# Linear attention with a routed expert layer: turns 4 to 19 of the attention in another order, their output rows turned in two halves

## The chip, the cores and the metric

The kernel runs on one core of a Trainium2 chip. Its engines are TensorE (PE, whose weight loads are listed as PEld), VectorE (DVE), ScalarE (ACT), GpSimd (POOL) and SyncE (SP), which issues most of the transfers. The metric is the device time of one execution in microseconds (us), less is better.

## The reference

A linear attention with a forget gate per channel (4 batches, 8 heads, 768 steps, 48 channels a head) makes one row of 384 numbers for each of 3072 tokens. An expert layer follows: each token goes to the one of 8 experts with the largest gate logit.

```
f = 1 / (1 + exp(-f_logit))
for t in range(S):
    state = f[:, :, t, :, None] * state + einsum('bhd,bhe->bhde', k[:, :, t], v[:, :, t])
    y[:, :, t] = einsum('bhd,bhde->bhe', q[:, :, t], state)
x = y as rows of tokens (3072 x 384)
logits = x @ w_gate; e_idx = argmax(logits)
for each expert e, on its tokens:
    out = gate_w * sigmoid(x @ w_output_gate)[e] * (relu(x @ w1[e]) @ w2[e])
```

## The kernel before

**Attention.** The steps are cut into chunks of 128 tokens: 4 batches of 6 chunks are 24 chunks in a row, and the loop `for t in range(last + 1)` makes one *turn* for each. Heads stand in pairs on the partitions (NP = 4 pairs of 64 rows). A turn holds work on several chunks, since each chunk goes through a pipeline:

- `pre(t + 2, ...)`, `pre(t + 3, "s")`: gates and their running products two or three chunks ahead. `s` and `f` are sigmoids on ACT from the loaded `f_t` (f into the single PSUM buffer `f_ps`), `scan_p` and `scan_i` are scans on DVE over `f_ps`, `mul_q` and `mul_k` multiply q and k by them on POOL, `ends` is a small copy on ACT.
- `qk(t)`: scores of the chunk on PE into two `a_ps` tiles. `mask` copies them to `at`: one half by ACT and then POOL (affine_select), the other by DVE.
- `kn_tr(t)`, `evac_kn(t)`: k with tokens on partitions, turned on PE and copied by ACT. The last chunk of a batch (t = 5, 11, 17, 23) has neither, nor a state product.
- `out_y(t - 1)` = `out_state` (q with the carried state) and `out_at` (scores with v) on PE. Their sums stand in half a PSUM bank each: `y_ps[0]` in the bank `two`, `y_ps[1]` in the bank `one`.
- `state(t - 1)`: product of k and v on PE into `s_ps`, the other half of the bank `one`. `state_upd` on DVE adds it to the carried state.
- `evac_y`: two copies on ACT of the outputs into `xt`. `x_tr(t - 2)` turns them into rows of tokens on PE (the right operand `turn` also yields the gate logits, 112 columns in all), and `evac_x` copies these on ACT.
- `route`, `slots` (every second or fourth turn): which expert each token goes to, on DVE, with a few small products on PE into the other half of the bank `two` (the rank products). `scatter`: POOL writes the rows of 128 tokens into the list of their experts in `xs_dram`, one scatter a turn from turn 7 on, more from turn 20 (`T_END`) on. With the first 16 tiles counted (`T_TOP`), a vote on DVE names the largest expert, whose w1 is then loaded.

The order in which the program is written is the order on each engine: `chain` ties every instruction of PE, DVE, ACT and POOL to the one before it on its engine. The transfers of SP run through one queue, in which the next one is issued when the eighth before it has landed. `clear` writes empty rows into the lists ahead of the scatters; only tiles that are known to stand elsewhere are declared apart from them, and the scatter of tile 3 waits for the second set of four writes. The tile framework lets an instruction wait for readers and writers of the same PSUM bank on other engines: `state_upd` waits for the copy of `one`, the rank products wait for that of `two`.

**Hand-over and experts.** In the last turn the reload of the first 256 tokens of the largest expert (`first_x`) waits for the first 16 scatters. `x_early_turn` and `x_early` turn and split them (DVE, ACT), and `mm1_early` is the first expert product (tile `h_ps`). From there on PE multiplies for the experts, one after another.

Of the kernel before, what the change touches and what calls it, by code (L numbers as in the profile page):

```python
# [21 lines left out]
C = 128  # L22
NCH = S // C
NP = H // 2
# [6 lines left out]
EARLY = 256  # L31
T_TOP = 16
T_END = 20
AHEAD = 8
KC = DM // 128
KF = F // 128
# [96 lines left out]
def attention(ctx, tc, nc, k, kpool, rt, q01, k01, f01, q23, k23, f23, v, wg, xs_dram, r, ex):  # L133
# [104 lines left out]
    def hot(t):  # L238
        return 0 <= t < len(order)
# [37 lines left out]
    def state(t):  # L277
        b, c = order[t]
        if c == NCH - 1:
            return  # L280
        for h in range(H):
            g, r0 = h // 2, 64 * (h % 2)
            nc.tensor.matmul(s_ps[r0:r0 + 64, g, 0:D], kn[t][:, 64 * h:64 * h + 64],  # L283
                             v_t[b][:, c, 64 * h:64 * h + D],
                             start=(h < 2), stop=(h >= 6), skip_group_check=True)

    def state_upd(t):
        b, c = order[t]
        if c == NCH - 1:
            return  # L290
        end = r.pend[:, t * NP:t * NP + NP].unsqueeze(2).broadcast_to([128, NP, D])
        scomp[t] = states[t % 2]
        new, kv = scomp[t][:, :, 0:D], s_ps[:, :, 0:D]
        if c == 0:
            nc.vector.tensor_tensor(out=new, in0=kv, in1=end, op=ALU.mult)
        else:
            nc.vector.tensor_tensor(out=stmp, in0=kv, in1=scomp[t - 1][:, :, 0:D], op=ALU.add)
            nc.vector.tensor_tensor(out=new, in0=stmp, in1=end, op=ALU.mult)
# [29 lines left out]
    def evac_y(t, halves=(1, 0)):  # L328
        if t not in xt:
            xt[t] = wk.tile([128, NP, C], F32, name="xt")  # L330
        for i in halves:
            nc.scalar.copy(out=xt[t][:, i::2, :], in_=yps[t][i])

    def x_tr(t):

        xps[t] = psB.tile([128, 512], F32, name="x_ps")[:, 0:NP * XW].rearrange("p (g e) -> p g e", e=XW)
        for g in range(NP):
            nc.tensor.matmul(xps[t][:, g, :], xt[t][:, g, :], turn[:, g, :], start=(g == 0), stop=(g == NP - 1))  # L338

    def evac_x(t):  # L340
        if t % 4 == 0:
# [22 lines left out]
    dq, pq = [], []  # L364
# [110 lines left out]
    def pre(t, *names):  # L475
        if hot(t):
            for nm in names:
                if nm not in done[t]:
                    done[t].add(nm)
                    pre_of[t][nm]()  # L480
# [26 lines left out]
    for gi, n in enumerate(RG):  # L507
        ends[t0 + n - 1] = (gi, t0, n)
        t0 += n
    for t in range(last + 1):  # L510
        ready = len(pq)
        more = 1 if t < T_END else 0

        fill(more)
        if hot(t - 2):
            evac_y(t - 2, (1,))
        if t not in (0, 2):
            pre(t + 2, "f")
        if hot(t - 2):
            evac_y(t - 2, (0,))  # L520
            state_upd(t - 2)
        if t == 2:
            pre(4, "f")
            pre(3, "ends")
        pre(t + 1, "mul_k")
        if t + 1 == last:
            done_sb.close()
            ex.open_early()
        fill(more)
        if t > 1:  # L530
            pre(t + 2, "scan_p")
        qk(t)
        mask(t, 1)
        mask(t, 0)
        pre(t + 2, "scan_p", "scan_i")
        fill(more)
        kn_tr(t)
        if t == 0:
            warm_up(nc, k, one, 6)
        if t == last:  # L540
            run_pq(ready)
        if hot(t - 2):
            x_tr(t - 2)
        evac_kn(t)
        pre(t + 2, "mul_q", *(("ends",) if t != 1 else ()))
        if hot(t - 2):
            evac_x(t - 2)
        if t == last:
            route(*ends[t - 2])
            drain()  # L550
        fill(more)
        if T_END <= t < last:
            fill(8)
        pre(t + 3, "s")
        if t == last:
            done_ps.close()
            ex.open_early_psum()
        if hot(t - 1):
            out_y(t - 1)
        if hot(t - 1):  # L560
            state(t - 1)
        if t == last:
            hand_over()
            break
        run_pq(ready)
        if t >= T_END:
            pre(t + 2, "mul_k")
        if t >= T_SCAT:
            scatter(1 if t < T_END else 2)

        b, c = divmod(t - 3, NCH)
        if t >= 3 and b + 2 < B and c in (0, 2, 4):
            if c == 4:
                load(b + 2, [("v", 0, 2)])
            load(b + 2, [("kq" if t == 3 else "fkq", c, c + 2)])
            if t == 3:
                ex.clear(3)
            if c == 4:
                load(b + 2, [("v", i, i + 2) for i in range(2, NCH, 2)])
        fill(2 if more else 10)  # L580
        fill(2 * more)
        if t - 2 in ends:
            route(*ends[t - 2])
        if t >= T_END:
            scatter(2)
            if len(ex.apart) == T_TOP:
                ex.tokens_in(0, 0, EARLY // TS)
                ex.load_rest(0)
        if t + 1 == last:
            drain()  # L590
            assert ex.xq
            ex.split(1, 0, 0)
# [600 lines left out]
```

## Time and profile before

| what | value |
|---|---|
| median of 3 runs | 352.92 us (352.49 to 352.97) |
| the profiled execution | 353.29 us, span from first to last instruction 351.6 us |
| PE busy | 339.4 us, 97% of the span |
| DVE, ACT, POOL busy | 250.0, 202.0, 209.8 us (71%, 57%, 60%) |
| turns of the attention | the first product of turn 0 at 9.2 us, of turn 4 at 25.75 us, of turn 20 at 97.16 us |

The shares are means over stages with different limits. The change touches the stretch from 25.75 to 97.16 us, which is why the rows below are cut by turn. Times in them count from the first instruction.

### The profile page before, as it was taken

What the parts mean: (1) busy time and instruction counts of PE and PEld (TensorE: products, weight loads), DVE (VectorE), ACT (ScalarE), POOL (GpSimd) and SP (SyncE); (2) the same over time, 40 slices, a digit from 0 to 9 for tenths busy, and PEclk for the clock granted to TensorE, in tenths of its full rate; (3) what the DMA queues carried; (4) which work ended last, traced back from release to release, by engine and by line L of the source; (5) the groups of instructions that cost most, each with busy time, mean ns of one, the idle gap of its engine ahead of it and who ended that gap; (6) DMA issues with size and microseconds to landing.
All of it is one profiled execution on the core that took longest, in us unless ns stands there. A gap on an engine that the chain in (4) does not pass through costs nothing.

```text
span 351.6 us, 8639 instructions
## 1 busy us (share of the span) xinstructions
PE 339.4 (97%) x3039; PEld 317.5 (90%) x3039; DVE 250.0 (71%) x495; ACT 202.0 (57%) x507; POOL 209.8 (60%) x250
## 2 busy tenths in 40 slices
PE   7899999999999899999999999999999999999991
PEld 2698988898988799999989999999999999999991
DVE  6998989898998676668766675766667666655600
ACT  3576866776766561455754752672673672775410
POOL 8786698999988461000674475276276276278521
PEclk9999999999999999999999999999999999999997
DMA  8999999999928927997683393495484484420101
GB/s 254 350 359 357 296 301 261 261 279 261 276 71 278 297 85 129 282 234 183 185 243 86 110 284 84 139 245 132 139 223 138 140 217 143 140 76 28 60 31 38
DMA packets 75204, 67.63 MB, mean 192 GB/s; under 512 B 30813, under 2 KB 69481, under 8 KB 75152
## 3 DMA queue, kind: packets, MB, share of 16 engines
q1 hardware_dynamic: 70576, 57.34, 60.4%
q0 software_dynamic: 4576, 9.66, 8.1%
q8 instruction: 26, 0.43, 0.5%
q14 instruction: 26, 0.21, 0.2%
HBM read 54.04 MB, written 13.46 MB: 192 GB/s over the span
## 4 chain that ended last, share of the span: by engine, by line
PE 84%; DMA 4%; DVE 3%; issue 3%; POOL 2%; ACT 1%; SPq 0%; POOLq 0%; DVEq 0%; ACTq 0%
PE h_ps L810 32%; PE y_ps L830 25%; PE x_ps L338 5%; PE a_ps L250 5%; PE y_ps L844 5%; PE two_ps L318 3%; PE kn_ps L267 3%; PE one_ps L318 2%; PE two_ps L310 2%; PE one_ps L283 2%; DMA xs_dram<-xn,slot 2%; DMA f_t<-in_f 1%; DVE p L214 1%; DMA first_x<-xs_dram 1%; POOL out L874 1%
## 5 line engine op out<-in xcount | busy, mean ns | idle before, releaser
L863 POOL DMA_INDIRECT out<-yr,dst x83 | 90.3, 1088 | 70.8 <-ACT yr L862 44.9
L810 PE MATMUL h_ps<-xh,w1h 128*128 128x400 f32 (+6 forms) x192 | 65.4, 341 | 0.0
L810 PE MATMUL h_ps<-xh,w1l 128*128 128x400 f32 (+6 forms) x192 | 65.4, 340 | 0.0
L810 PE MATMUL h_ps<-xl,w1h 128*128 128x400 f32 (+6 forms) x192 | 65.3, 340 | 0.0
L815 DVE SCALAR_TENSOR_TENSOR hl<-h_ps,hh 128x256 fp32r<-128x256 f32 (+6 forms) x72 | 39.0, 544 | 32.8 <-ACT hh L814 32.6
L814 ACT ACTIVATE hh<-h_ps 128x256 fp32r<-128x256 f32 (+6 forms) x72 | 34.5, 482 | 42.6 <-PE h_ps L810 41.4
L830 PE MATMUL y_ps<-hh,w2h 128*128 128x256 f32 (+4 forms) x168 | 56.1, 334 | 0.0
L830 PE MATMUL y_ps<-hl,w2h 128*128 128x256 f32 (+4 forms) x168 | 56.0, 334 | 0.0
L830 PE MATMUL y_ps<-hh,w2l 128*128 128x256 f32 (+4 forms) x168 | 56.0, 334 | 0.0
L673 DVE TENSOR_TENSOR w1l<-w1r,w1h 128x768 fp32r<-128x768 f32 x31 | 29.7, 959 | 16.7 <-ACT w1h L672 16.5
L810 PEld LDWEIGHTS h_ps<-xh,w1h 128*128 128x128 f32 x192 | 36.1, 188 | 0.8
L810 PEld LDWEIGHTS h_ps<-xl,w1h 128*128 128x128 f32 x192 | 36.1, 188 | 0.7
L810 PEld LDWEIGHTS h_ps<-xh,w1l 128*128 128x128 f32 x192 | 36.1, 188 | 0.7
L228 POOL TENSOR_TENSOR q_t<-q_t,p 128x512 f32<-128x512 f32 x24 | 30.5, 1272 | 3.5 <-DVE p L214 2.3
L830 PEld LDWEIGHTS y_ps<-hh,w2h 128*128 128x128 f32 x168 | 31.7, 189 | 0.7
L830 PEld LDWEIGHTS y_ps<-hh,w2l 128*128 128x128 f32 x168 | 31.7, 189 | 0.7
L830 PEld LDWEIGHTS y_ps<-hl,w2h 128*128 128x128 f32 x168 | 31.7, 189 | 0.7
L355 POOL DMA_INDIRECT xs_dram<-xn,slot x24 | 24.5, 1022 | 10.8 <-issue 5.9
L673 DVE TENSOR_TENSOR w2l<-w2r,w2h 128x768 fp32r<-128x768 f32 x31 | 29.6, 954 | 1.4 <-ACT w2h L672 0.6
L777 ACT CAST xh<-xr 128x400 fp32r<-128x400 f32 (+6 forms) x24 | 12.2, 517 | 31.2 <-DVE xr L771 30.1
L250 PE MATMUL a_ps<-q_t,k_t 64*128 64x128 f32 x384 | 27.9, 285 | 2.1 <-DVE k_t L225 1.1
L225 POOL TENSOR_TENSOR k_t<-k_t,i 128x512 f32<-128x512 f32 x22 | 28.2, 1280 | 2.6 <-DVE i L221 1.4
(168 smaller groups left out, 738.5 us busy)
## 6 DMA issues: line engine op xcount, KB each, us to landing
w1r<-in_w SPq DMA_DIRECT2D x32, 384.0 KB, 4.0
w2r<-in_w SPq DMA_DIRECT2D x32, 384.0 KB, 3.5
v_t<-in_v SPq DMA_DIRECT2D x12, 512.0 KB
xs_dram<-empty SPq DMA_DIRECT2D x8, 401.0 KB, 10.5
f_t<-in_f SPq DMA_DIRECT2D x6, 512.0 KB, 4.0
q_t<-in_q SPq DMA_DIRECT2D x6, 512.0 KB
k_t<-in_k SPq DMA_DIRECT2D x6, 512.0 KB, 10.2
f_t<-in_f SPq DMA_DIRECT2D x12, 192.0 KB, 9.3
```

The lines of the kernel that those rows point to most:

```text
L225: eng.tensor_tensor(out=k_t[i][:, :, sl], in0=k_t[i][:, :, sl], in1=d["i"], op=ALU.mult)
L228: nc.gpsimd.tensor_tensor(out=q_t[i][:, :, sl], in0=q_t[i][:, :, sl], in1=d["p"], op=ALU.mult)
L250: nc.tensor.matmul(aps[t][par][:, g, :], k_t[b % 2][r, g, sl], q_t[b % 2][r, g, sl], start=(g == 0), stop=(g == NP - 1))
L318: nc.tensor.matmul(yps[t][g % 2][r0:r0 + 64, g // 2, :], v_t[b][:, c, 64 * h:64 * h + 64], at[t][:, h % 2, g, :], start=((first or c == 0) ...
L338: nc.tensor.matmul(xps[t][:, g, :], xt[t][:, g, :], turn[:, g, :], start=(g == 0), stop=(g == NP - 1))
L355: i = nc.gpsimd.indirect_dma_start(out=xs_dram, out_offset=bass.IndirectOffsetOnAxis(ap=r.slot[:, t:t + 1], axis=0), in_=xn[t // 4][:, t % ...
L673: (eng or self.nc.vector).tensor_tensor(out=to(lo), in0=of(t), in1=to(hi.bitcast(F32)), op=ALU.subtract)
L810: nc.tensor.matmul(ps[:, 0:n], a[:, c, cs], b, start=(i == 0), stop=(i == 3 * KC - 1))
L814: nc.scalar.activation(out=hi, in_=ps[:, 0:n], func=AF.Relu)
L815: nc.vector.scalar_tensor_tensor(out=lo, in0=ps[:, 0:n], scalar=0.0, in1=hi.bitcast(F32), op0=ALU.max, op1=ALU.subtract)
L830: self.nc.tensor.matmul(self.ys[d][:, c0:c0 + n], a, b, start=(f == 0 and i == 0 and part == 0), stop=(f == KF - 1 and i == 2), skip_group ...
L863: self.other_rows(self.nc.gpsimd.indirect_dma_start(out=self.out.rearrange("n (q w) -> (n q) w", q=NQ), out_offset=bass.IndirectOffsetOnAx ...
```

## The change

Turns 4 to 19 (the fifth to the twentieth) run `next_turn` in place of the old body, which becomes `old_turn` and serves turns 0 to 3 and 20 to 23. In `next_turn` the outputs of the chunk before stand right behind `qk`, then the state's product, and the rows and k are turned last. The copies of outputs and the state's update stand in the same turn as their products, the copy of the bank `one`, which the state's product shares, second. `f` is computed a turn earlier. `closed` keeps the old body from doing an update a second time. `x_tr(t, 2)` makes each product in two halves of 64 tokens, 64 weight columns each, into the partitions 0 to 63 and 64 to 127.

```diff
+T_NEXT = 4
...
-    def x_tr(t):
+    def x_tr(t, parts=1):
...
+        n = C // parts
         for g in range(NP):
-            nc.tensor.matmul(xps[t][:, g, :], xt[t][:, g, :], turn[:, g, :], start=(g == 0), stop=(g == NP - 1))
+            for a in range(0, C, n):
+                nc.tensor.matmul(xps[t][a:a + n, g, :], xt[t][:, g, a:a + n], turn[:, g, :], start=(g == 0),
+                                 stop=(g == NP - 1), skip_group_check=True)
...
-    for t in range(last + 1):
-        ready = len(pq)
-        more = 1 if t < T_END else 0
-
+    def old_turn(t, ready, more):
         fill(more)
-        if hot(t - 2):
+        if hot(t - 2) and t - 2 not in closed:
             evac_y(t - 2, (1,))
...
-        if hot(t - 2):
+        if hot(t - 2) and t - 2 not in closed:
             evac_y(t - 2, (0,))
             state_upd(t - 2)
...
+    def next_turn(t, ready):
+
+        if t - 2 not in closed:
+            evac_y(t - 2)
+            state_upd(t - 2)
+        pre(t + 1, "mul_k")
+        pre(t + 2, "f", "scan_p")
+        qk(t)
+        mask(t, 1)
+        mask(t, 0)
+        pre(t + 2, "mul_q", "ends")
+        pre(t + 3, "s")
+        fill(1)
+        out_y(t - 1)
+        state(t - 1)
+        pre(t + 2, "scan_i")
+        fill(2)
+        evac_y(t - 1, (0, 1))
+        state_upd(t - 1)
+        closed.add(t - 1)
+        pre(t + 3, "f")
+        x_tr(t - 2, 2)
+        kn_tr(t)
+        evac_x(t - 2)
+        evac_kn(t)
...
+        if T_NEXT <= t < T_END:
+            next_turn(t, ready)
+        else:
+            old_turn(t, ready, more)
```

Below, rows of the built programs in their order on an engine; line numbers after the change are 1, 4 or more higher.

PE in turn 9, before (from `qk` to `state`; a_ps are the scores, kn_ps the turned k, x_ps the turned outputs, one_ps and two_ps the banks):

```order
L250 MATMUL a_ps<-q_t_99,k_t_101 128x128 x8
L267 MATMUL kn_ps<-ident,k_t_101 128x128 x4
L338 MATMUL x_ps<-turn,xt 128x112 x4
L310 MATMUL two_ps<-q_t_99,state_107 64x128 x2
...
L318 MATMUL two_ps<-at,v_t 64x128 x2
...
L283 MATMUL one_ps<-v_t,kn 64x48 x8
```

PE in turn 9 after the change:

```order
L251 MATMUL a_ps<-q_t_99,k_t_101 128x128 x8
L311 MATMUL two_ps<-q_t_99,state_107 64x128 x2
...
L319 MATMUL two_ps<-at,v_t 64x128 x2
...
L284 MATMUL one_ps<-v_t,kn 64x48 x8
L341 MATMUL x_ps<-turn,xt 64x112 x8
L268 MATMUL kn_ps<-ident,k_t_101 128x128 x4
```

The turning of rows and of k moved from behind the scores to the end of the turn, and the rows' four products became eight of 64 partitions.

ACT over one turn, before (from the copy of masked scores of turn 9 on; start_p is `s`, f_ps is `f`):

```order
L255 ACTIVATE at<-a_ps 128x512
L275 COPY kn<-kn_ps 128x512
L231 COPY pend<-p 128x4
L345 COPY lgp<-x_ps 128x64
L346 COPY xn<-x_ps 128x384
L202 ACTIVATE start_p_176<-f_t_102 128x4
L204 COPY p<-start_p_176 128x1
L332 COPY xt<-one_ps 128x2x128
L209 ACTIVATE f_ps<-f_t_102 128x4x127
L332 COPY xt<-two_ps 128x2x128
```

ACT over the same turn after the change:

```order
L256 ACTIVATE at<-a_ps 128x512
L232 COPY pend<-p 128x4
L203 ACTIVATE start_p_176<-f_t_102 128x4
L205 COPY p<-start_p_176 128x1
L333 COPY xt<-two_ps 128x2x128
L333 COPY xt<-one_ps 128x2x128
L210 ACTIVATE f_ps<-f_t_102 128x4x127
L349 COPY lgp<-x_ps 128x64
L350 COPY xn<-x_ps 128x384
L276 COPY kn<-kn_ps 128x512
```

`s` moved ahead of both copies of the outputs, `f` behind them, and the copies of the rows and of k to the end, in the order of PE.

## Rows read from the trace of the kernel before

**Rows 1.** Windows from turn to turn: length, busy (instructions), clock, DMA share, GB/s.

```profile
47.93:52.56 4.63, 4.63 (x80) 4.18 (x76) 4.04 (x7) 3.31 (x10) 4.42 (x5) 1.00 1.08 326
...
61.90:66.07 4.17, 4.17 (x64) 3.60 (x60) 3.89 (x8) 3.23 (x10) 3.92 (x5) 1.00 1.11 275
...
74.74:79.58 4.84, 4.84 (x85) 4.36 (x81) 3.81 (x7) 3.50 (x11) 4.66 (x6) 1.00 1.08 274
...
84.21:88.71 4.50, 4.32 (x77) 3.79 (x73) 3.91 (x7) 2.76 (x9) 4.30 (x5) 1.00 1.09 276
...
92.89:97.16 4.27, 4.27 (x69) 3.97 (x67) 3.81 (x7) 3.45 (x11) 4.08 (x6) 1.00 0.91 282
97.16:101.79 4.63, 4.63 (x80) 4.17 (x77) 4.01 (x13) 3.19 (x10) 3.72 (x5) 1.00 0.20 74
```

**Rows 2.** Timeline of PE in turn 9: start, length, engine, line, work.

```profile
49.02 0.66 PE L267 MATMUL kn_ps<-ident,k_t 128*128 128x128 f32 x4
49.52 1.04 PE L338 MATMUL x_ps<-turn,xt 128*128 128x112 f32 x8
50.49 0.33 PE L310 MATMUL two_ps<-q_t,state 64*64 64x128 f32 x2
...
51.09 0.44 PE L318 MATMUL two_ps<-at,v_t 128*64 128x128 f32 x4
...
51.58 0.39 PE L318 MATMUL two_ps<-at,v_t 128*64 128x128 f32 x4
...
52.01 0.62 PE L283 MATMUL one_ps<-v_t,kn 128*64 128x48 f32 x16
```

**Rows 3.** Line of the state's product: ns of one, shortest, median, longest.

```profile
L283 PE MATMUL one_ps<-v_t,kn x320: 206/222/222, 15.8 to 115.4; 128*64 128x48 f32 x160
```

**Rows 4.** Timeline of PE in turn 17; in brackets idle time and releaser.

```profile
85.56 1.15 PE L338 MATMUL x_ps<-turn,xt 128*128 128x112 f32 x8 [0.18 <-ACT xt L332]
```

**Rows 5.** Timeline of POOL: scatters, mul_k (L225), mul_q (L228).

```profile
58.41 1.01 POOL L355 DMA_INDIRECT xs_dram<-xn,slot  x1 [1.13 <-DMA q_t<-in_q]
59.45 1.29 POOL L225 TENSOR_TENSOR k_t<-k_t,i 128x512 f32<-128x512 f32 x1
...
65.63 1.27 POOL L228 TENSOR_TENSOR q_t<-q_t,p 128x512 f32<-128x512 f32 x1
...
69.94 1.27 POOL L228 TENSOR_TENSOR q_t<-q_t,p 128x512 f32<-128x512 f32 x1
...
80.45 1.01 POOL L355 DMA_INDIRECT xs_dram<-xn,slot  x1 [0.56 <-DVE misc L297]
...
94.50 1.28 POOL L225 TENSOR_TENSOR k_t<-k_t,i 128x512 f32<-128x512 f32 x1
```

**Rows 6.** Timeline of ACT around s(18) (L202) in turn 15.

```profile
77.51 0.49 ACT L346 COPY xn<-x_ps 128x384 f32<-128x384 f32 x1
78.15 0.21 ACT L202 ACTIVATE start_p<-f_t 128x4 f32<-128x4 f32 x1
...
79.49 0.37 ACT L332 COPY xt<-one_ps 128x256 f32<-128x256 f32 x1 [0.85 <-PE one_ps L283]
```

**Rows 7.** Timeline of SP: issue of the loads of f for turns 18, 19.

```profile
66.91 1.21 SPq L190 DMA_DIRECT2D f_t<-in_f  x2
```

**Rows 8.** Chain that ended last, at the hand-over: start, length, what.

```profile
106.60 6.56 DMA xs_dram<-xn,slot
...
114.78 3.59 DMA first_x<-xs_dram
```

**Rows 9.** Timeline at the hand-over: SP's issue of w1, PE's last and first products.

```profile
103.32 2.86 SPq L647 DMA_DIRECT2D w1r<-in_w  x4
...
118.58 0.28 PE L310 MATMUL f_ps<-q_t,state 64*64 64x128 f32 x2
...
119.43 0.38 PE L810 MATMUL h_ps<-xah,w1h 128*128 128x256 f32 x1 [0.55 <-ACT xah L777]
```

More of the change, by code (lines that the diff above doesn't have):

```diff
@@ L561, in attention @@
             state(t - 1)
+    def next_turn(t, ready):
[22 more added lines that the diff above has]
+        evac_kn(t)
+    closed = set()
+    for t in range(last + 1):
+        ready = len(pq)
+        more = 1 if t < T_END else 0
+        if T_NEXT <= t < T_END:
+            next_turn(t, ready)
+        else:
+            old_turn(t, ready, more)
         if t == last:
```

## The prediction

> **What bounds the kernel now.** I read the sums by turn first: one window from the first product of a turn to that of the next. In a full turn TensorE (PE) is busy for the whole window, 4.63 of 4.63 us, at a granted clock of 1.00, while VectorE (DVE), ScalarE (ACT) and GpSimd (POOL) are busy for 4.04, 3.31 and 4.42 us [rows 1]. So the order of work on PE sets the pace of turns 4 to 19, and the reader should look for three things: what a turn costs PE, where PE waits, and what else would stop it if it were quicker.
>
> The timeline of PE in turn 9 gives the cost by block, from start to start: qk 1.09, kn_tr 0.50, x_tr 0.97, out_state 0.60, out_at 0.92, state 0.55, together 4.63 us (the turn's ends are those of its window) [rows 1, 2]. Nothing waits in it. PE waits in a turn without kn_tr: in turn 17 x_tr stands 0.18 us for the copy of outputs on ACT, and PE is busy for 4.32 of 4.50 us [rows 1, 4].
>
> Right behind PE stands POOL. From the fourth scatter, at 58.41 us, it works almost without a gap, at 69.94 - 65.63 = 4.31 us a turn [rows 5]. PE takes (97.16 - 61.90) / 8 = 4.41 us for a turn there [rows 1], so POOL keeps up with PE and could not keep up with a much quicker one.
>
> **The change on PE, step by step.** The order within a turn is now qk, out_state, out_at, state, x_tr in halves, kn_tr.
>
> *x_tr.* From x_tr to out_state it is 0.97 us: eight passes, of which the last is followed by a change of tile shape. With a pitch of 0.11 us (7 x 0.11 = 0.77) the change of shape costs 0.20 us. In halves it is eight pairs of passes of 64 weight columns, which stand in different columns of the array. Two rows show such pairs: state has 8 pairs at (0.62 - 0.222) / 7 = 0.057 us, with 48 moving columns [rows 2, 3], and out_at has 4 pairs in 52.01 - 51.58 = 0.43 us, 0.109 us a pair, with 128 columns [rows 2]. For 112 columns I take 0.109 x 112 / 128 = 0.096 us; the bounds are 0.057 and 0.109.
>
> *The changes of shape.* Before, state's last pass is followed by qk 0.55 - 7 x 0.057 = 0.15 us later. A new turn is qk 1.09, out_state 0.60, out_at 0.92, state 8 x 0.057 = 0.46 (x_tr has its shape and follows at once), x_tr 7 x 0.096 + 0.20 = 0.87, kn_tr 0.50 - 0.11 + 0.20 = 0.59: 4.53 us, **0.10 us less**.
>
> The Trainium skill, page TensorEngine Tiling (Array Packing), section Key Properties, says that a change of tiling mode drains the engine and a change of tile does not. The trace agrees: 0.15 to 0.20 us at each of the four changes in a full turn [rows 2]. By this rule the new order gains nothing by itself in a full turn, since it has four changes too.
>
> *Turns without kn_tr* (5, 11, 17) lose a change of shape and the 0.18 us wait, since x_tr then works on outputs that were copied a turn earlier: 4.53 - 0.59 = 3.94 instead of 4.50 us, 0.55 less. *Rank products* (turns 7, 11, 15, 19) stood between state and qk, two changes around 0.21 us (4.84 against 4.63 [rows 1]); they now follow kn_tr in its shape: some 0.1 us less, estimated.
>
> *Seam.* Turn 20 has the old order again, so kn_tr(20) comes right after qk, while ACT's last work of turn 19 is the copy of kn_tr(19), behind f and the copies of x. I take 0.35 us lost there (bounds 0 and 0.6, one kn_tr block). Without any other bound this makes 13 x 0.10 + 3 x 0.55 + 4 x 0.1 - 0.35 = **3.0 us**.
>
> **What stops it.** A transfer or POOL fixes three places.
> 1. The fourth scatter starts at 58.41 us after 1.13 us of idle [rows 5]. The code makes it wait for the four writes of empty rows (only tiles 0 to 2 are declared apart from them), and the DMA share is 1.08 or more in the windows up to turn 17 [rows 1], so DMA is full. Those don't come earlier with PE. Then mul_k(12) ends at 59.45 + 1.29 = 60.74, so turn 12 can lead by no more than 1.1 us (it began at 61.90).
> 2. s(18) on ACT needs a load of f that was issued at about 67.8 us [rows 7]; it ran at 78.15, 0.15 us after its predecessor's end (77.51 + 0.49) [rows 6], with nothing else to wait for. I read this as just in time; the load itself doesn't move, since DMA is full. In the new order the copies of turn 14's outputs stand behind it on ACT, where the old order had made them. Two small operations (0.21 each, about 0.4) and the first copy (0.37 [rows 6]) end near 78.9, the rank products of turn 15 use the copied bank and take until 79.2, so turn 16 leads by 79.58 - 79.2 = 0.4 us. All that was gained before is lost here.
> 3. From turn 16 on a turn takes 4.53, 3.94, 4.07 (turn 18 is of the kind of turn 12, 4.17 - 0.10) and 4.07 (4.27 - 0.2) [rows 1], so that turn 20 would begin at 95.8 us. POOL's mul_k(20) ends at 94.50 + 1.28 = 95.8 too [rows 5]. So the lead is 97.16 - 95.85 = 1.3 us, and after the seam **0.95 us**, which turns 21 to 23, unchanged, carry on.
>
> **Hand-over to the experts.** The first product of the experts waits 0.55 us for its input, while PE's last product of attention starts at 118.58. That input hangs on a chain of its own: 16th scatter at 106.60, landing 6.56 us later, reload of the tokens (last one 3.59 us), transpose, cast [rows 8, 9]. The scatter shares DMA with the first expert's w1, issued at 103.32; before that, DMA is only 0.20 busy [rows 1, 9]. The vote that frees w1 stands on DVE in turn 20 and comes about 1.3 us earlier, so w1 uses idle DMA, and the scatter lands earlier, although POOL issues it only some 0.3 us earlier. Bounds: 0.3 us (the issue alone) and 1.6 us. PE could use up to 0.95 + 0.55 = 1.5 us. I take 1.2 us, nearer to the upper end, because the 6.56 us are mostly shared DMA. From there on PE is the bound, and what is gained stays.
>
> **The sum**: 353.29 - 1.2 = 352.1 us for an execution like the profiled one (span 351.6). That one lies 0.37 us above the median of the runs, 352.92, so I predict **351.7 us**. Below about 0.7 us (0.2%) a measurement can't tell a difference from none.
>
> **Rivals.**
> - *The tokens' chain doesn't move.* Only POOL's 0.3 us arrives: 352.6, no difference. For it: POOL is saturated, the chain already ended last by 0.55 us. Against: idle DMA ahead of w1.
> - *The load of f doesn't bind.* Then POOL alone limits; its idle time of 0.56 us at 80.45 [rows 5], a wait for the slots that turn 15 counts, shrinks too. PE's lead at turn 20 is up to 1.9 us, after the seam 1.5, with 0.55 more at the hand-over: 350.9.
> - *The eight additional passes aren't hidden* (place: x_tr). If pairs don't run together, a turn has 16 x 0.096 = 1.53 instead of 8 x 0.11 = 0.89 us, 0.64 more: 13 x 0.54 + 3 x 0.09 + 0.35 = 7.6 us, 360.5. It decides from a pitch of a pair above 0.125 us. Against it: out_at's pairs at 0.109 us.
>   The Trainium skill, same page, section Instruction Overhead, gives each matmul about 60 cycles. With 2.4 GHz that would be an estimated 0.2 us a turn for eight more passes and would turn the gain of a full turn into a loss of 0.1 us. The trace of state's pairs, 0.057 us for two passes, speaks against it as a cost on top.
> - *ACT's queue makes it slower.* y's copies now stand behind s, and state_upd behind the copies. If the load of f for turn 18 lands d later than now, turn 16 starts at 0.4 - d, with everything after. From d = 1.9 us on the kernel is slower by 0.7 us; with 2.5 us: 354.2. For it: every us counts fully. Against: the DMA queue is always full, its order is unchanged, and only the scatters' times move.
>
> **Chances.** Forecast 0.50 (351.3 to 352.2), tokens' chain 0.26, load not binding 0.12, passes 0.05, ACT's queue 0.07. Those make faster 0.60 (the forecast's upper edge and some of the second rival cancel), same 0.28, slower 0.12. The range goes from 350.8, the second rival with a little more at the hand-over, to 352.9, no change, which leaves out the slow cases.
>
> **What would show it.** In a full turn of the new order PE's window is 4.53 us with x_tr as 16 passes in about 0.87 us up to kn_tr; turns 5 and 17 near 3.94. POOL from 58 us on stands where it stood. s(18) starts at 78.1 and turn 16 at 79.2. Turn 20 starts near 95.9 and has a wait of kn_tr. The first h_ps starts near 118.2. The prediction is wrong if x_tr's pairs have a pitch over 0.11 us, if turn 16 leads by more than 1 us, or if the tokens land at 118 as before.

## The result: slower, and the profile after

The changed kernel takes 356.35 us (median of 16 runs, 353.86 to 359.61) where the kernel before, run beside it, takes 353.1 (352.49 to 354.32): a ratio of 1.0078 with a 95% interval of [1.0049, 1.0107]. This ratio and those below leave out runs more than 1.5% above the fastest of the same kernel (here 359.23 and 359.61 us). The forecast was 351.7 us, with a range up to 352.9. The runs also lie much further apart than before, 5.75 us against 1.83. The profiled execution took 354.17 us (span 352.4), so it is one of the quick ones; a second profiled execution, of the run f1 below, took 357.69.

The order on PE does in a full turn what was forecast. Windows of the changed kernel, columns as in [rows 1]: turns 9, 11, 13, 17 and 19, each from its first product of scores to the next turn's.

```profile
47.17:51.70 4.53, 4.53 (x85) 3.92 (x85) 4.04 (x8) 3.64 (x13) 4.32 (x5) 1.00 1.09 330
56.23:61.42 5.19, 4.47 (x86) 3.78 (x86) 3.62 (x7) 2.56 (x10) 3.25 (x6) 1.00 1.03 271
65.58:70.05 4.47, 4.20 (x70) 3.68 (x69) 3.51 (x6) 3.66 (x11) 4.27 (x6) 1.00 1.09 282
...
84.95:89.60 4.65, 4.35 (x82) 3.70 (x81) 4.03 (x7) 2.93 (x9) 4.42 (x5) 1.00 1.09 269
93.67:98.38 4.71, 4.31 (x75) 3.88 (x74) 3.80 (x7) 3.93 (x13) 4.41 (x6) 1.00 0.65 211
```

Turn 9 is 4.53 us long and has no gap. The others have 0.27 to 0.72 us in which PE is not busy. Before, PE had no idle time there but 0.18 us each in turns 11 and 17 [rows 4]. The timeline of PE in turn 9 shows the new step; columns as in [rows 2].

```profile
49.78 0.62 PE L284 MATMUL one_ps<-v_t,kn 128*64 128x48 f32 x16
50.23 0.95 PE L341 MATMUL x_ps<-turn,xt 128*64 128x112 f32 x16
51.12 0.66 PE L268 MATMUL kn_ps<-ident,k_t 128*128 128x128 f32 x4
```

State's product takes 0.45 us to the next block and the rows in halves 0.89 us, for 0.46 and 0.87 in the prediction.

First products of turns and of the experts, in us from the first instruction, read from the timelines of PE:

| kernel | turn 4 | 5 | 9 | 11 | 12 | 16 | 17 | 18 | 20 | 23 | first h_ps |
|---|---|---|---|---|---|---|---|---|---|---|---|
| before | 25.75 | 30.38 | 47.93 | 57.19 | 61.90 | 79.58 | 84.22 | 88.71 | 97.16 | 111.21 | 119.43 |
| after | 25.71 | 30.58 | 47.17 | 56.23 | 61.42 | 79.74 | 84.95 | 89.60 | 98.38 | 112.44 | 120.47 |
| after, second execution (f1) | 25.74 | 30.60 | 47.19 | 56.26 | 61.81 | 80.67 | 86.90 | 92.65 | 101.71 | 115.76 | 123.89 |

Up to turn 11 the changed kernel gains 0.96 us. From there to turn 20 it loses 2.18 in one execution and 5.48 in the other. From turn 20 on nothing more is lost, and from the first h_ps to the end of the span it takes 231.9 us, before 232.2. So all of the loss, and the spread of the runs too, as far as two executions show it, lies in turns 11 to 19. These are the places where PE stands still there, in brackets the idle time and its releaser:

```profile
59.21 0.44 PE L319 MATMUL two_ps<-at,v_t 128*64 128x128 f32 x4 [0.62 <-issue]
...
66.78 0.49 PE L251 MATMUL a_ps<-q_t,k_t 64*128 64x128 f32 x4 [0.27 <-issue]
...
79.51 0.18 PE L423 MATMUL two_ps<-ohb,upper 128*128 128x32 bf16 x1 [0.26 <-ACT xt L333]
81.64 0.32 PE L311 MATMUL one_ps<-q_t,state 64*64 64x128 f32 x1 [0.28 <-issue]
88.69 0.98 PE L341 MATMUL x_ps<-turn,xt 128*64 128x112 f32 x14 [0.30 <-issue]
96.58 0.38 PE L284 MATMUL one_ps<-v_t,kn 128*64 128x48 f32 x6 [0.40 <-issue]
```

One of the six is a wait for ACT. The other five have no releaser, and they fall into the middle of a group of equal passes: at 59.21 half of the 16 passes of out_at are done, and the others, from the same line and on the same tiles, come after 0.62 us of idle PE. "issue" says only that the profile shows nothing that was waited for. The page's list of DMA queues shows what the stops have in common; packets, MB and share. First the kernel before, then the changed one.

```profile
q8 instruction: 26, 0.43, 0.5%
```

```profile
q8 instruction: 27, 0.44, 0.6%
```

Queue 8 carries packets of 16,384 bytes, and there are 26 of them for 6,153 instructions of PE in the trace, 27 for 6,411: one packet more for 258 instructions more. The halves added 16 instructions (eight passes and their weight loads) to each of 16 turns, 256 in all. Counted in the trace's records of PE, the instructions at 59.21, 66.78, 81.64, 88.69 and 96.58 stand 255, 513, 256 and 255 records apart (513 are two blocks; a record can be missing). So the stops are the first instructions of blocks of 256. For each block the trace gives two distances: how long after the start of the block before its packet starts (**wait**), and how long after the packet's end the block's first instruction runs (**behind**). Here are the sixth to the eleventh block, which are first used between 58 and 106 us, in us (where no stop marks the start of a block, it is counted in records, to about 0.1 us; a negative wait is a packet that started ahead of the block before):

```
                           wait                               behind
block                 6    7    8    9   10   11       6    7    8    9   10   11
before             3.86 2.38 2.86 4.08 3.66 0.79    2.56 5.06 2.96 2.86 3.70 5.62
after              5.46 4.82 4.11 5.50 4.35 5.32    1.40 1.44 1.35 1.33 1.42 1.37
after (f1)         5.87 5.39 4.82 6.23 5.35 5.61    1.37 1.34 1.21 1.16 1.49 1.54
f4 rows whole      4.47 4.20 3.42 6.07 6.61 1.64    2.16 2.88 2.92 1.38 1.46 5.59
h4 halves alone    5.89 5.97 5.36 5.24 4.97 4.27    1.32 1.50 1.45 1.48 1.73 2.27
h3 depth 7         4.32 3.51 3.76 5.07 2.03 2.97    1.53 2.12 1.96 1.41 3.18 3.11
h1 depth 6         0.89 1.39 2.79 4.19 1.21 2.81    5.18 4.45 2.88 1.76 3.86 3.40
g1 both remedies   2.45 1.19 2.35 2.87 -.05 2.73    3.47 4.77 2.94 2.96 5.03 3.12
f2 depth 4         0.72 0.27 2.36 1.78 0.30 0.88    5.19 6.62 3.20 7.29 6.46 5.14
```

In the changed kernel every one of these blocks starts 1.33 to 1.44 us behind its packet, before none nearer than 2.56 us. PE ran as fast as its program arrived: (96.58 - 59.21) / 5 = 7.47 us for 256 instructions. From the sixth to the eleventh block the kernel before uses one in 7.98 us on average (63.26 to 103.16), so its program came in time.

The Trainium skill, page Runtime: NRT & Kernel Launch, section Instruction fetch mechanics, says that an engine's program is refilled in blocks of 256 instructions through a DMA queue of the engine's own. The trace agrees with that, by its 16,384 bytes and its 256 records. The Trainium skill, in the same section, calls the crossing of a block mostly hidden. In the kernel before it was hidden, in the changed one it isn't, with stops of 0.27 to 0.62 us.

### The profile page after: what moved, and what is told of

The parts are those of the page before. It is cut to its first block, busy times and chain, and to the rows that moved or that the text cites. A ratio compares the mean times of both kernels' runs of the same rounds, so it can differ in the third digit from the quotient of the medians.

```text
span 352.4 us, 8894 instructions
## 1 busy us (share of the span) xinstructions
PE 338.1 (96%) x3167; PEld 314.5 (89%) x3167; DVE 250.4 (71%) x495; ACT 201.2 (57%) x507; POOL 210.4 (60%) x250
## 4 chain that ended last, share of the span: by engine, by line
PE 81%; DMA 10%; issue 3%; DVE 3%; ACT 1%; POOL 1%; POOLq 0%; ACTq 0%; DVEq 0%
PE h_ps L846 32%; PE y_ps L866 24%; DMA f_t<-in_f 10%; PE a_ps L251 5%; PE y_ps L880 5%; PE x_ps L341 4%; PE two_ps L319 3%; PE kn_ps L268 2%; PE one_ps L319 2%; PE two_ps L311 2%; PE one_ps L284 2%; POOL out L910 1%; DVE p L215 1%; DVE i L222 1%; POOL k_t L226 0%
## 5 line engine op out<-in xcount | busy, mean ns | idle before, releaser
L215 DVE TENSOR_TENSOR_SCAN p<-f_ps,start_p 128x511 f32<-128x511 f32 x21 | 26.8, 1275 | 4.1 <-ACT start_p L203 2.1
```

What stands on the lines that cost most here:

```text
L215: nc.vector.tensor_tensor_scan(out=flat(d["p"])[:, 1:n], data0=flat(d["f"])[:, 0:n - 1], data1=sp[:, 1:n], initial=sp[:, 0:1], op0=ALU.mul ...
```

## Experiments

**Theory (instruction supply).** In turns 4 to 17 DMA is full, and a packet of instructions queues behind the loads. A full turn has 171 instructions at 4.53 us after the change, which use a block in 6.8 us (256 / 171 x 4.53), and 155 at 4.63 us before, 7.6 us a block; the counts are from the traces, and the expectations below, which take 176 and 160, have both about 0.2 us too short. The supply doesn't keep up, PE stops, and how long depends on the queue, so runs spread. **Rival (ACT's queue).** It is the prediction's fourth rival: s waits on ACT for a load of f, and the copies of outputs behind it hold up PE. The changed kernel has a trace of that too, a wait of 1.95 us at s(18); columns as in [rows 6].

```profile
76.55 0.20 ACT L232 COPY pend<-p 128x4 f32<-128x4 f32 x1
78.70 0.21 ACT L203 ACTIVATE start_p<-f_t 128x4 f32<-128x4 f32 x1 [1.95 <-DMA f_t<-in_f]
79.00 0.19 ACT L205 COPY p<-start_p 128x1 f32<-128x1 f32 x1
79.10 0.37 ACT L333 COPY xt<-two_ps 128x256 f32<-128x256 f32 x1
```

Ratios are to the kernel before, run on the same chip.

### First chip: e1 to e4

These four ran on a chip on which the kernel before takes 404.63 us (400.94 to 407.54). There PE stops in the expert layer as well (in e1 for 26.2 us at the products of y_ps, with no releaser), and the granted clock there is 0.85 to 0.92 from 160 us on, so the expected times can't be held to it; the ratios and the traces of the attention can.

**e1: rows whole in the new order.**

```diff
-        x_tr(t - 2, 2)
+        x_tr(t - 2)
```

> The new order, with the rows turned whole again (four products a turn, not eight). Theory (instruction supply): PE takes its program in blocks of 256 instructions, one packet of 16 KB each, and in turns 10 to 19 of the changed kernel it stands still until 1.33 to 1.44 us after the end of the packet. The halves added 16 instructions to each of 16 turns (256 in all, one block), so a block is used up in 6.6 us of a full turn's pace (256 / 176 x 4.53) where it lasted 7.4 us before (256 / 160 x 4.63). Without the halves a block lasts 7.4 us again, there are 26 packets, the idle time put down to 'issue' in PE's turns 10 to 19 falls from 1.9 us to under 0.5, and the time is 352.0 to 353.5 us with a narrow spread. Rival (ACT's queue): what costs is the new order, in which the copies of outputs stand behind s on ACT and s waits for loads of f that land later; then the halves don't matter, and the time stays within 1 us of the changed kernel's median, 355.5 to 357.5.

Measured: 404.37 us, ratio 0.9972 [0.9933, 1.0012]. 26 packets. Up to turn 19 the stops with no releaser sum to 1.26 us, not under 0.5, at the ninth and the tenth block. It is repeated as f4.

**e2: halves in the old order.** `next_turn` is never called.

```diff
-        if T_NEXT <= t < T_END:
+        if t < 0:
...
-            x_tr(t - 2)
+            x_tr(t - 2, 2 if T_NEXT <= t < T_END else 1)
```

> The old order in all turns, with the rows of turns 4 to 19 turned in halves. Theory (instruction supply): 27 packets of instructions, blocks of 176 instructions a turn against a supply of about 7.4 us for 256, so PE stands still in the middle of groups of equal products, with no releaser, after 50 us; turns take up to 5.1 us there (176 / 256 x 7.4) in place of 4.63. Slower than before by 2 to 4 us: 355 to 357.5, with a wide spread. Rival (ACT's queue): the old order has the copies of outputs in their old place, PE's own work in a full turn is the same within 0.02 us (one change of shape more, 0.10 less for the eight pairs), so the time is that of before, 352.5 to 353.8.

Measured: 406.24 us, 1.0042 [1.0005, 1.0079]; stops with no releaser of 0.72, 0.42 and 0.52 us in the old order. It is repeated as h4.

**e3: copies of outputs ahead of s.**

```diff
-        pre(t + 3, "s")
         fill(1)
...
-        pre(t + 3, "f")
+        pre(t + 3, "s", "f")
```

> The changed kernel, but s of turn t + 3 stands behind the copies of outputs on ACT, directly ahead of f. Rival (ACT's queue): the waits of s for the loads of f (2.16 us in turn 11, 1.95 us in turn 15) no longer hold the copies, the rank products and the state's update; the lead of PE that was lost at turns 12 and 16 stays, and the time is 351.5 to 352.5. Theory (instruction supply): PE still asks for 176 instructions a turn, so the stops with no releaser stay, 0.3 to 0.9 us for each block from the sixth on; the time stays within 1.5 us of the changed kernel's median of 356.35, 355 to 357.5, with a wide spread.

Measured: 410.27 us, 1.0134 [1.0078, 1.019]; stops of 5.7 us in all and no wait for ACT. The rival alone is out. It is repeated as g3.

**e4: no loads of v for two batches.** Those batches use the v of the other two, so this part of the result is left out.

```diff
-                load(b + 2, [("v", 0, 2)])
+                v_t[b + 2] = v_t[b]
...
-                load(b + 2, [("v", i, i + 2) for i in range(2, NCH, 2)])
```

> The changed kernel without the loads of v for the batches 2 and 3 (3.1 MB in six transfers issued between 57 and 91 us); their products use v of the batches 0 and 1, so that part of the result is left out. All other work is the same. Theory (instruction supply): DMA is less than full in part of the turns 11 to 19, packets of instructions wait less behind the loads, so stops with no releaser become shorter there and none is left from the point on where the DMA share falls below 1; 351.0 to 353.0, and the spread narrows. The rival (ACT's queue) expects a gain too, since loads of f land earlier, but the stops with no releaser would stay as they are, as the number of instructions is the same.

Measured: 404.5 us, 1.0019 [0.9981, 1.0057], no faster as a whole. In its attention the sixth block is still at the limit (1.31 us behind its packet). The blocks after it, with part of the loads gone, stand 2.27 to 5.88 us behind theirs. PE has no stop between 60 and 96 us, and turn 20 begins at 95.18 us, where e1 to e3 begin it at 99.9 to 101.6. The same 171 instructions a turn go through when less stands ahead of them in DMA.

### Second chip: f1 to f4

The kernel before takes 352.8 us here (352.26 to 353.98).

**f1: the changed kernel again.**

> The changed kernel itself, on the chip of the three kernels beside it, as their measure. Both theories: 1.005 to 1.012 times the time of before. Theory (instruction supply): in its trace the start of each block of 256 instructions from the sixth to the eleventh stands 1.2 to 1.7 us behind the end of its packet, and PE's idle time put down to 'issue' in turns 10 to 19 sums to 1.5 us or more. Rival (ACT's queue): the waits of s and the copies behind it account for what turns 12 and 16 lose, and stops with no releaser come out small or elsewhere.

Measured: 357.27 us (352.73 to 358.54), 1.0083 [1.0053, 1.0114]. Its stops in turns 11 to 19:

```profile
59.78 0.44 PE L319 MATMUL two_ps<-at,v_t 128*64 128x128 f32 x4 [1.17 <-issue]
67.63 0.49 PE L251 MATMUL a_ps<-q_t,k_t 64*128 64x128 f32 x4 [0.81 <-issue]
74.78 0.74 PE L341 MATMUL x_ps<-turn,xt 128*64 128x112 f32 x10 [0.26 <-issue]
83.59 0.32 PE L311 MATMUL one_ps<-q_t,state 64*64 64x128 f32 x1 [1.39 <-issue]
...
91.74 0.98 PE L341 MATMUL x_ps<-turn,xt 128*64 128x112 f32 x14 [1.40 <-issue]
99.90 0.38 PE L284 MATMUL one_ps<-v_t,kn 128*64 128x48 f32 x6 [0.67 <-issue]
```

They are the same instructions as in the first execution, with the sixth one, in the eighth block, now seen too. They sum to 5.70 us against 1.87, 3.83 more, and this execution is 3.52 us longer. There is no wait for ACT among them.

**f2: 4 loads under way in place of 8.** A dependence makes each transfer of SP wait for the fourth before it (from the first load of the third batch to all but the last two).

```diff
+    for n in range(FIRST, LAST):
+        tc.add_manual_dep(sp[n], sp[n - DEPTH].name, ...)
```

> The changed kernel with 4 loads under way in SP's queue in place of 8, from the second half's loads on (turns 2 to 18); the same instructions and bytes. Theory (instruction supply): a packet of instructions waits behind what the queue has handed to its DMA engine; with half of it the packets start 2 to 3.5 us after the start of the block before, in place of 4.1 to 5.5, the blocks stand ready, and the stops with no releaser in turns 10 to 19 go (under 0.3 us together). 0.985 to 0.997 of the changed kernel's time on this chip, that is 0.992 to 1.003 of before. Rival (ACT's queue): the loads land no earlier with a shallower queue, since DMA is full either way; s waits as before or longer, and the time is that of the changed kernel or above it (1.005 to 1.015 of before).

Measured: 355.37 us, 1.0064 [1.0037, 1.0091], outside what the theory expected. The packets do what it says (wait 0.27 to 2.36 us, no stop with no releaser). But DMA is no longer full (230 GB/s between 70 and 82 us, 276 in f1), the loads land later, and the rival's wait opens, on ACT in turn 15 and then on PE:

```profile
80.58 0.21 ACT L204 ACTIVATE start_p<-f_t 128x4 f32<-128x4 f32 x1 [3.91 <-DMA f_t<-in_f]
```

```profile
81.39 0.18 PE L424 MATMUL two_ps<-ohb,upper 128*128 128x32 bf16 x1 [2.35 <-ACT xt L334]
```

Right behind that wait TensorE's granted clock is at its lower level, 1.2 GHz, for 3.4 us (the last three columns of a window are clock, DMA share and GB/s), and turn 16 takes 6.18 us (81.61 to 87.79) where it takes 4.54 without any stop (g1 below). So a part of what f2 loses in this execution is the clock's.

```profile
82.60:86.00 3.40, 3.40 (x43) 2.85 (x41) 3.21 (x5) 1.96 (x7) 2.98 (x4) 0.50 1.09 214
```

**f3: the kernel before with 4 loads under way.**

> The kernel before with the same shallower queue (4 loads under way). Control for the run beside it. Theory (instruction supply): before, no block stood closer than 2.56 us behind its packet where 1.33 to 1.44 are needed, so there is nothing to gain on a chip where that holds: 0.997 to 1.003. If the shallow queue makes this one as much faster as the changed kernel, then it is the loads and not the instructions that it helps, which speaks for the rival.

Measured: 353.96 us, 1.0023 [1.001, 1.0037]: no gain, a small loss by loads that come late (1.08 us at x_tr in turn 16, behind an s that waited 2.80 us on ACT).

**f4: rows whole again.**

> The new order with the rows turned whole, beside the changed kernel on one chip. Theory (instruction supply): 160 instructions in a full turn as before the change, so the stops with no releaser are smaller than in the changed kernel in the same place: 0.985 to 0.996 of the changed kernel's time, 0.994 to 1.002 of before. Rival (ACT's queue): the order costs, not the halves; the same time as the changed kernel within 0.3%.

Measured: 354.47 us (352.02 to 356.43), 1.0042 [1.0017, 1.0066]: 0.9922 of f1's median (354.47 / 357.27), as expected, but still slower than before, which was not. A full turn takes 4.68 us (43.29 to 47.97), so this order gains nothing there with rows whole, and two blocks are late with only 155 instructions a turn:

```profile
87.82 0.32 PE L319 MATMUL two_ps<-at,v_t 128*64 128x128 f32 x1 [0.63 <-issue]
```

So the number of instructions is a part of the cause, not all of it: the packets of these two waited 6.07 and 6.61 us.

### Third chip: g1 to g4

The kernel before takes 353.07 us here (352.46 to 356.5).

**g1: copies first and 6 loads under way.** The edits of e3 and of f2, with `DEPTH = 6`.

> The changed kernel with both remedies: s of turn t + 3 behind the copies of outputs on ACT, and 6 loads under way in SP's queue in place of 8. What the runs so far show: with 4 loads under way a packet of instructions starts 0.3 to 2.4 us after the block before and nothing stops for it, but DMA is no longer full (share 0.86 to 0.99) and the loads of f land 2 us later, which the copies behind s on ACT pass on to PE. Combined theory (instruction supply sets turns 11 to 19 of the changed kernel, ACT's queue is the next limit behind it): packets start 1.5 to 3.5 us after the block before, stops with no releaser under 0.5 us in all, copies don't wait for loads, turn 20 begins at 95.8 to 97.0 us and the time is 0.993 to 1.000 of before. If the instruction supply alone were the cause, the depth alone (1.0064) should have been enough; if ACT's queue alone were, the copies ahead of s with 8 loads under way (run beside this one) should be enough.

Measured: **351.23 us (350.84 to 351.54), 0.9942 [0.9928, 0.9956]**: faster than both kernels, and its six runs lie within 0.7 us. From turn 4 to turn 19 PE has one idle time, in turn 4; the other two shown are the seam in turn 20 and the wait for the tokens:

```profile
27.44 0.33 PE L312 MATMUL two_ps<-q_t,state 64*64 64x128 f32 x2 [0.26 <-DVE state L300]
...
96.44 0.65 PE L269 MATMUL kn_ps<-ident,k_t 128*128 128x128 f32 x4 [0.51 <-ACT kn L277]
...
117.75 0.39 PE L846 MATMUL h_ps<-xah,w1h 128*128 128x256 f32 x1 [0.68 <-ACT xah L813]
```

Turn 20 begins at 94.69 us, 2.47 ahead of before (expected was 95.8 to 97.0), and DMA stays nearly full (share 1.00 to 1.07 from 45 to 97 us).

Set beside g1, the first execution of the changed kernel is longer in the turns with its six stops (11, 13, 15, 16, 17 and 19) by 1.03, 0.54, 0.46, 0.67, 0.71 and 0.51 us, 3.92 in all, and in turns 12, 14 and 18 by 0.14 together. The profile shows 2.13 us of idle time for these stops: the modelled end of the pass ahead of a stop covers the rest. The 0.46 us are the stop that waits for ACT, so the rival had a share of at least an eighth in this execution.

**g2: the same with 4 loads under way.**

> The same with 4 loads under way. Combined theory: no stop for instructions at all, but loads land up to 2 us later (DMA share 0.86 to 0.99), so f(t), v or k itself may be late for PE: 0.996 to 1.004 of before, and faster than the same depth with s ahead of the copies (1.0064), whose worst wait, 2.35 us for the copies in turn 15, is gone. Instruction supply alone: the same as that one, since no packet waits in either.

Measured: 354.46 us (352.44 to 358.92), 1.0039 [1.0009, 1.0069]. No stop with no releaser; qk waits 0.69 us for a load of k itself and 1.2 us for mul_k behind such loads. Against f2 (1.0064) the medians are near and the intervals overlap, so that the copies help at this depth is not shown by times; the 2.35 us wait is gone from the trace.

**g3: copies first alone, 8 loads under way.**

> The changed kernel with s behind the copies of outputs and 8 loads under way. Theory (instruction supply): PE's blocks come as late as in the changed kernel; 1.005 to 1.014 of before, stops with no releaser of 3 us or more in turns 10 to 19. Rival (ACT's queue): 0.993 to 0.999.

Measured: 357.24 us (354.49 to 359.16), 1.0094 [1.0054, 1.0134]; its stops sum to 3.4 us, and behind the longest, 1.68 us, the clock is at 0.50 for 3.4 us (84.2 to 87.6) as in f2. The rival alone is out on this chip too.

**g4: rows whole, copies first, 6 loads under way.**

> Rows turned whole, s behind the copies, 6 loads under way: 160 instructions in a full turn. Combined theory: no stop for instructions; PE needs 4.68 us in a full turn (as in the run with whole rows) instead of 4.53, and wins only in the turns without k to turn. Turn 20 at 96.5 to 98 us, 0.996 to 1.003 of before, and slower than the halves with both remedies by 0.2 to 0.6%.

Measured: 353.73 us, 1.0018 [1.0008, 1.0028]: no stop, turn 20 at 96.93 us. The halves are worth 0.76% (1.0018 against 0.9942) once they are supplied, a little more than expected.

### Fourth chip: h1 to h4

The kernel before takes 353.81 us here (352.88 to 358.04).

**h1: 6 loads under way alone.** `DEPTH = 6`, with s ahead of the copies as in the change.

> The changed kernel with 6 loads under way in SP's queue, s ahead of the copies of outputs as in the change. Instruction supply alone as the cause: as fast as with both remedies, 0.993 to 0.996 of before, with turn 20 at 94.5 to 95.5 us. Both causes: packets of instructions in time (no stops with no releaser beyond 0.5 us in all), but s waits for loads of f in turns 11 and 15, the copies behind it let PE wait 0.3 to 1.2 us there, and the time is 0.996 to 1.000 of before. The prediction's forecast of 1.3 us of lead at turn 20 after the pin of s(18) would then be seen at last: turn 16 between 78.5 and 79.5 us.

Measured: 352.57 us (350.86 to 356.1), 0.9965 [0.9934, 0.9996]. The depth alone turns the loss into a gain. The time lies at the lower edge of what both causes together expected. No stop with no releaser is left in turns 4 to 19, and turn 20 begins at 95.12 us, as "supply alone" had it. It doesn't separate the two cleanly, though: against expectation the loads land earlier too (that of f for s(18) at 76.99 us, 78.62 in the changed kernel), so s(18) ran at 77.07 and its wait cost PE nothing. Of the lead of 1.71 us at turn 23 (109.50 for 111.21) only 0.82 arrive at the experts, since the tokens' chain is now late:

```profile
118.61 0.38 PE L847 MATMUL h_ps<-xah,w1h 128*128 128x256 f32 x1 [1.44 <-ACT xah L814]
```

Behind this wait too the clock is at 0.50, from 120.8 to 124.2 us. From the first h_ps to the end it takes 233.7 us in place of 232.2; the profiled execution (354.11 us) lies 1.5 us above the median.

**h2: the kernel before with 6 loads under way.**

> The kernel before with 6 loads under way: the control for the shallower queue. No block of instructions was late there, so theory (instruction supply) expects 0.998 to 1.003 of before. If it gains 0.4% or more by itself, the gain of the run with both remedies isn't the change's.

Measured: 353.51 us, 0.998 [0.9951, 1.001]. The depth gains nothing that can be told without the change.

**h3: copies first, 7 loads under way.**

> The changed kernel with s behind the copies and 7 loads under way, between 6 (0.9942, no stop) and 8 (1.0094, stops of 3 to 4 us). Theory (instruction supply): the wait of a packet grows with what is handed to the DMA engines ahead of it, so packets start 2 to 4.5 us after the block before and single stops of 0.2 to 1 us come back: 0.994 to 1.003 of before, with a wider spread than the 0.7 us at 6.

Measured: 353.61 us (352.72 to 356.56), 1.0006 [0.9976, 1.0036]; stops of 0.90 and 0.17 us are back, with waits of 2.03 to 5.07 us in the list; the longer stop is the start of the fourth block, at 46.26 us, whose packet waited 5.85 us. So the wait goes with the depth, and from 6 up the time with it: ratios of 0.9942, 1.0006 and 1.0094 at 6, 7 and 8 (g1, h3, g3), on two chips. At 4 (g2, 1.0039) it is the loads that come late.

**h4: halves in the old order again.**

> The old order with the rows of turns 4 to 19 in halves, on the chip of these runs. Theory (instruction supply): 176 instructions in a full turn with 8 loads under way, so blocks come late after 50 us, stops with no releaser of 1.5 to 5 us in all, and the time is 1.004 to 1.012 of before with a spread of 3 us or more. Rival (the order is what costs): 0.998 to 1.002.

Measured: 356.63 us (353.76 to 359.18), 1.0063 [1.0029, 1.0098]. The old order with 256 more instructions is as slow, and as spread, as the changed kernel. Its stops:

```profile
60.62 0.33 PE L311 MATMUL two_ps<-q_t,state 64*64 64x128 f32 x2 [0.65 <-issue]
69.20 0.49 PE L251 MATMUL a_ps<-q_t,k_t 64*128 64x128 f32 x3 [1.25 <-issue]
77.11 0.61 PE L284 MATMUL one_ps<-v_t,kn 128*64 128x48 f32 x13 [0.28 <-issue]
...
93.04 0.61 PE L284 MATMUL one_ps<-v_t,kn 128*64 128x48 f32 x14 [1.12 <-issue]
```

They are other instructions than in the changed kernel, again the first of blocks, 1.32 to 1.73 us behind their packets.

## Why the prediction was wrong

**The step that failed** is the list in "What stops it": "A transfer or POOL fixes three places." A fourth limit was left out, the transfer that carries PE's own program. The prediction priced the halves' passes only as time in the array ("the eight additional passes aren't hidden ... if pairs don't run together"), found them free, and took the full 3.0 us up to the pins. As time in the array they are free, 0.89 us for the step. As 16 instructions a turn through a full DMA they cost more than the whole change gives: h4 shows the cost without the order (1.0063), g1 the gain without the late program (0.9942). The halves aren't the only part that pays: the order alone had two late blocks in f4 (1.0042). (The prediction's price for passes that don't pair, 7.6 us, takes off the 0.10 us of a full turn a second time; that rival didn't come true.)

**Was it to be seen?** In part. Before, the nearest block stood 2.56 us behind its packet, and 1.2 to 1.7 us are needed, so about 1 us was left; the change takes 7.6 - 6.8 = 0.8 us from a block in full turns. That alone says tight, not late. What it doesn't say is that the packets' waits grow from at most 4.08 to 5.5 us. No row of the usual views has these distances; the page has only the count of packets.

**PE's sums held.** The full turn is 4.53 us as forecast. Turn 5 takes 34.52 - 30.58 = 3.94 us, and in g1 turn 17 takes 86.41 - 82.47 = 3.94: forecast 3.94. It needs both parts of the change: with the order alone a full turn takes 4.68 us (f4), with the halves alone 4.67 (h4, 47.92 to 52.59). What the sum left out is the other seam, at turn 4, which takes 4.87 us in the changed kernel for 4.63 before, since the outputs wait for the state's update (0.26 us, as in the row of g1 above).

**Pin 1** (fourth scatter at 58.41): it ran at 58.51, and mul_k(12) ended at 60.84.

```profile
58.51 1.01 POOL L359 DMA_INDIRECT xs_dram<-xn,slot  x1 [1.92 <-DMA f_t<-in_f]
59.55 1.29 POOL L226 TENSOR_TENSOR k_t<-k_t,i 128x512 f32<-128x512 f32 x1
```

Turn 12 began only at 61.42, since PE stopped in turn 11 for its sixth block. In h1, without that stop, mul_k(12) ended at 59.09 + 1.28 = 60.37 and turn 12 began at 60.42: there the pin binds, and turns 12 and 13 take 4.33 and 4.31 us, POOL's own pace as the prediction has it (4.31). In g1 the scatter ran at 57.66, and mul_k(12) ended 0.77 us ahead of turn 12 (59.99 for 60.76). The pins are times of transfers, and these moved with the depth.

**Pin 2** (load of f, turn 16 at 79.2): in the profiled execution the load landed 0.56 us later than before (78.62 for 78.06) and turn 16 began at 79.74. That is the fourth rival's sum to the hundredth: 79.58 - (0.4 - 0.56). So this rival was there, with 0.26 us of idle PE behind it; but PE was late by its program too, so the exact match is luck. The second execution loses more without it, and with it removed (e3, g3) the loss stays.

**Pin 3** (mul_k(20) at 95.8 us) didn't bind in the changed kernel: PE came at 98.38. With the supply mended turn 20 began at 95.12 (h1) and 94.69 (g1), each 0.05 us behind the end of mul_k(20) (93.78 + 1.29 = 95.07 and 93.36 + 1.28 = 94.64). So POOL sets this place as the prediction says, but it stands earlier, as pin 1 does: leads of 2.04 and 2.47 us for the 1.3 forecast.

**The seam** (0.35 us, bounds 0 and 0.6) shows only with a lead: turn 20 takes 4.63 us in the changed kernel, 4.95 in h1 and 5.29 in g1, so 0.32 and 0.66 lost, the second above the bound.

**The hand-over** (1.2 us, bounds 0.3 and 1.6): 0.82 in h1 and 1.68 in g1. The size is near, the mechanism is not. The prediction let an earlier w1 use idle DMA, so that the 16th scatter lands sooner after its issue, and the issue move by 0.3 us only. These are the scatter and the reload in h1, then in g1; columns as in [rows 8].

```profile
105.21 6.70 DMA xs_dram<-xn,slot
...
113.85 3.70 DMA first_x<-xs_dram
```

```profile
104.74 6.43 DMA xs_dram<-xn,slot
...
112.83 3.86 DMA first_x<-xs_dram
```

The scatter takes as long as before (6.56 us), though w1 was issued 1.81 and 2.24 us earlier (101.51 and 101.08). What comes earlier is its issue, by 1.39 and 1.86 us. That the forecast of 1.2 us lies between the two is luck.

**The range and the chances.** Slower had 0.12, most of it on ACT's queue and the passes as array time. The kernel came out slower by a mechanism that no rival named.

**What stays open.** Why a packet waits 4.1 to 5.5 us in the changed kernel where it waited 2.4 to 4.1 us before (blocks 6 to 10) with the same 8 loads under way; f4, with 155 instructions, has waits over 6 us too. That a starving PE asks for the next block later would fit, but no run isolates it.

## What to carry to other kernels

Count the instructions that an edit adds to an engine, not only their time: where DMA is full, the engine's program shares it. A stop with no releaser in the middle of a group of equal instructions, at the same instruction in each execution, was here the sign of late program, and times that spread from run to run went with it. Fewer loads under way can mend it at no cost as long as DMA stays nearly full: here 6 in place of 8, while 4 were too few.

## What the runs showed of the hardware

- Between the end of a packet of 256 instructions and the first of them on a PE that stands waiting lie 1.16 to 1.73 us (19 late blocks of the two executions of the changed kernel, f4 and h4), and the packet itself takes 0.9 to 1.7 us.
- How long such a packet queues goes with the loads under way: in the six blocks of the list with 8 up to 6.6 us, with 7 up to 5.1 (5.85 in the fourth block of h3), with 6 up to 4.2, with 4 up to 2.4. DMA's share hardly tells 8 from 6: between 58 and 70 us it is 1.08 and 1.10 in the two executions of the changed kernel, 1.06 and 1.08 in g1 and h1.
- With 6 loads under way the load of f for s(18) landed earlier, at 76.99 and 76.62 us (h1, g1), than with 8: 78.06 before, 78.62 and 77.99 in the two executions of the changed kernel, 77.25 in g3. With 4 it landed at 80.50 (f2).
- The same program with late blocks ran in times up to 5.8 us apart; with both remedies, 0.7 us over six runs. The kernel before spread by 1.7 to 5.2 us on the same chips.
- Behind three long stops of PE (2.35 us in f2, 1.68 in g3, 1.44 in h1) TensorE's granted clock fell from 1.00 to 0.50, 2.4 to 1.2 GHz, for 3.4 us. In f2 the turn in which it fell took 6.18 us, for 4.54 in g1.
